# A margin for TensorE's order, small steps on two engines, 400 unread products and earlier squares in an attention and two-MoE kernel

## The chip, the cores and the metric

The kernel runs on one core of one Trainium2 chip. The metric is the device time of one execution in microseconds; the median of three runs is given. Engines are called TensorE (PE, its weight loads PEld), VectorE (DVE), ScalarE (ACT) and GpSimd (POOL). SyncE (SP) issues the DMAs.

## The reference, cut to what matters

```python
# q, k, v: (4, 8, 576, 64); M_prev: (4, 8, 64, 64); tokens: 4 * 576 = 2304, model width 8 * 64 = 512
scores = where(causal, -1e9, scale * q @ k^T)
local = softmax(scores) @ v
q_p = where(q > 0, q, exp(q) - 1) + 1
mem_out = (q_p @ M_prev) / (q_p . z_prev + 1e-6)
x = g * mem_out + (1 - g) * local            # g = sigmoid(beta); x: (2304, 512)

h = x @ w_in                                 # MoE1, 512 -> 2048
x = softplus(h) @ w_out                      # 2048 -> 512

h = x @ w_in2                                # MoE2
P = a0 + a1*h + a2*h^2 + a3*h^3
Q = 1 + |b0|*|h| + |b1|*h^2
out = (P / (Q + 1e-6)) @ w_out2
```

## The kernel before, in words

**Stages.** Attention is cut into seven passes, each a batch with a range of its query tiles (`PASSES`). A pass is cut into units of two or four heads: u0 to u5 in passes 0 to 2, which are computed in f32, and 16 later units in fp16 (a high and a low half for each value). Per unit there are scores, the mask with the row maximum, the exponential, a transpose of the probabilities and the product with v ("av" below), and beside it the memory part. The tokens that a pass finishes make a block for MoE1. Block 0's products are in f32 (128x256, 128 of them for each of the two matrices), those of the others in fp16 with three products for one. MoE2 follows over all 2304 tokens in 96 groups: 12 products of 384 columns for h (h1), then 9 of 512 columns for the output (h2).

**Weights.** The inputs are 64-bit values that the kernel takes apart on the chip: a piece of 128x512 comes as two words for each value, and VectorE makes f32 of it with one tensor_scalar and two scalar_tensor_tensor on integers (`bits`). There are 16 pieces of w_in and 16 of w_out for MoE1 (`w1_bits`, with `w1_load` for the DMA). Then `w1_stage2` squares every piece on ScalarE, with the sum of squares of each partition into a column of wacc1, takes the maximum of these with `w_scale` (which ends in `pmax`: a reduction over lanes on GpSimd and a product on TensorE) and splits each piece into two fp16 halves. The squares' unread full output goes to a_t[1]. In the trace these tiles are named w (pieces that belong to w_14 and others by number in the order), arena (one large buffer of which most tiles are cut), a (a_t), tiny (columns of scalars), gg and iog (the gate), bank (PSUM) and mask.

**What sets the order.** Every operation is first recorded in a program with a list of engines that can do it (`flex` records several) and a rank (`key`, for TensorE `pkey`; low goes first). `Program.order` then runs a list scheduler over a table of costs (`cost`, `LATENCY`, `BIAS`): each engine has a heap `wait` of operations whose inputs come at a known modelled time, and a heap `ready` ordered by rank. An operation that several engines may do goes to the one whose modelled end, weighted with the bias, is earliest. `emit` issues all instructions in the order that comes out, which is fixed then; so nearly all of them bear the line of `emit`: L426 before, L437 after (L439 and L441 before are L450 and L452 after). Each engine takes its own in that order and waits where an input isn't there. The ranks for TensorE: attention first by unit, then MoE1 by block, then MoE2 by group. `pmax` has the first rank of all; 120 unread products on a zero mask (`WARM`, rank 1e6) have the last.

VectorE and GpSimd share a port in the planner's costs: an operation of one gets longer while the other is working (`port`, `PORT`).

Of the kernel before, what the change touches and what calls it, by code (L numbers as in the profile page):

```python
# [24 lines left out]
LAG = 3  # L25
NLOW = 4

# [19 lines left out]
WARM = 120  # L47
FA32 = 3
# [81 lines left out]
def cost(eng, name, kw):  # L130
# [15 lines left out]
    if eng == "DVE":  # L146
        if name == "reciprocal":
            return 67 + 6.2 * n
        one = name in ("tensor_scalar", "tensor_copy", "memset") and not psum
        aps = sum(is_ap(kw.get(k)) for k in ("scalar", "scalar1", "scalar2", "scale"))  # L150
        return (77 if name == "tensor_tensor_reduce" else 67) + (0.52 if one else 1.042) * n + 62 * aps
# [19 lines left out]
class Program:  # L171
# [151 lines left out]
    def order(self):  # L323
# [13 lines left out]

        def release(o):
            o.cand = {"BULK"} if o.bulk and "SP" in o.alts else set(o.alts)
            for e in o.cand:  # L340
                heapq.heappush(wait[e], (o.ready, o.pkey if e == "PE" else o.key, o.idx))
# [8 lines left out]
        while len(done) < len(self.ops):  # L350
            best = None
            for e in engines:
                trim(ready[e])
                trim(wait[e])
                if ready[e]:
                    s = max(free[e], now[e])
                elif wait[e]:
                    s = max(free[e], wait[e][0][0])
                else:
                    continue  # L360
# [5 lines left out]
            now[e] = s  # L366
            while wait[e] and wait[e][0][0] <= s:
                _, k, i = heapq.heappop(wait[e])
                heapq.heappush(ready[e], (k, i))
# [6 lines left out]
            if t > s:  # L376
                heapq.heappush(wait[e], (t, k, i))
# [20 lines left out]
            if e in port and e in o.port:  # L398
# [57 lines left out]
def attn_moe_moe2(ctx, tc, q, k, v, m_prev, z_prev, beta, w1i, w1o, w2i, w2o, ca, cb, out):  # L456
# [123 lines left out]
    def tt(out, in0, in1, op, eng="VG"):  # L580
        kw = dict(out=out, in0=in0, in1=in1, op=op)
        P.flex(*[(e, "tensor_tensor", kw) for e, c in ((V, "V"), (G, "G")) if c in eng])

    def stt(out, in0, scalar, in1, op0, op1):
        V.scalar_tensor_tensor(out=out, in0=in0, scalar=scalar, in1=in1, op0=op0, op1=op1)
# [11 lines left out]
    def ts(out, in0, s1, s2, op0, op1=None):  # L597
# [3 lines left out]
        V.tensor_scalar(**kw)  # L601
# [765 lines left out]
    def w1_bits(which, pc):  # L1367
        r = w1_raw(which, pc)
        dst = w1_place(which, pc + 2, True)
        bits(r, dst.bitcast(U32))  # L1370

    def w1_stage2(which):
        for pc in range(16):
            A.activation(out=a_t[1][:, 768:1280], in_=w1_place(which, pc + 2, True), func=AF.Square, accum_out=wacc1[which][:, pc:pc + 1])
# [49 lines left out]
    for _ in range(WARM):  # L1424
        PE.matmul(out=bank[0][:, 0:256], lhsT=mask[:, 0:128], rhs=mask[:, 0:256], start=True, stop=True)
    early = EARLY(load, units, consts, lambda: batch_load(passes[0]))
# [273 lines left out]
```

## Time and profile before

| what | value |
|---|---|
| median of 3 runs | 1016.39 us (1015.85 to 1101.25) |
| profiled execution | 1013.9 us |
| its span, first to last instruction | 1011.8 us |
| mean granted clock of TensorE, as a share of full speed | 0.976 |
| busy: TensorE / VectorE / ScalarE / GpSimd | 94% / 86% / 71% / 47% |
| instructions on VectorE / ScalarE / GpSimd | 2182 / 1636 / 579 |

The times of stages and instructions below come from the profiled execution alone, whose own time is 2.1 us more than its span. A share of busy time is a mean over stages with different limits; the views by stage, the timelines of an engine and the lists of what it waited for are what tells them apart. An f32 product shows as two records in the trace.

### The profile page before, as it was taken

How to read it: one execution, taken by the hardware profiler on the slowest of the kernel's cores; microseconds unless marked ns; L12 is line 12 of the kernel's file. 1: busy time of each engine (PE TensorE's matmuls, PEld its weight loads, DVE VectorE, ACT ScalarE, POOL GpSimd, SP SyncE). 2: the span in 40 equal slices, each digit the busy share in tenths (PEclk: the TensorE clock that was granted, in tenths of full speed). 3: DMA queues.
4: the chain of work that ended last, by engine and by line, in shares of the span. 5: the costliest groups of instructions: out<-in, count | busy, mean ns of one | idle time of the engine just before them, and what ended most of it. 6: DMA issues, size and time to landing. Idle time of an engine off the chain costs nothing.

```text
span 1011.8 us, 22830 instructions
## 1 busy us (share of the span) xinstructions
PE 950.3 (94%) x8386; PEld 689.3 (68%) x8386; DVE 872.1 (86%) x2182; ACT 722.2 (71%) x1636; POOL 474.7 (47%) x579
## 2 busy tenths in 40 slices
PE   7776899999899999999799999999999999999998
PEld 6454587788788888888689899555555555555553
DVE  4989899899798888889769997988979889898886
ACT  4765896768676768777554444888788787887875
POOL 2434397933253343244225342564555455555443
PEclk9777899999999999999999999999999999999999
DMA  9997247688699888989997542000101000000000
GB/s 233 302 239 203 53 88 140 134 147 167 128 177 187 142 156 160 174 170 198 216 289 248 197 150 60 10 1 32 32 1 64 1 32 32 1 33 1 32 1 31
DMA packets 247584, 117.89 MB, mean 117 GB/s; under 512 B 218928, under 2 KB 225072, under 8 KB 247472
## 3 DMA queue, kind: packets, MB, share of 16 engines
q1 hardware_dynamic: 247472, 116.44, 50.6%
q8 instruction: 65, 1.06, 0.5%
q14 instruction: 47, 0.39, 0.1%
HBM read 63.45 MB, written 13.63 MB: 76 GB/s over the span
## 4 chain that ended last, share of the span: by engine, by line
PE 37%; DVE 9%; DMA 7%; issue 2%; POOL 2%; ACT 1%; SPq 0%; POOLq 0%; DVEq 0%; ACTq 0%
PE bank L426 37%; DVE arena L426 5%; DMA arena<-arena 2%; DVE bank L426 1%; DMA arena<-in_moe_w_out_dram 1%; DMA arena<-in_moe_w_in_dram 1%; POOL arena L426 1%; DMA arena<-a 1%; DVE gr L426 1%; ACT arena L426 1%; DMA w2d<-a 1%; DVE a L426 1%; DVE tiny L426 0%; DMA arena<-in_q_dram 0%; SPq L426 0%
## 5 line engine op out<-in xcount | busy, mean ns | idle before, releaser
L426 PE MATMUL bank<-arena,w 128*128 128x160 f16 (+3 forms) x4448 | 406.2, 252 | 0.7 <-ACT arena L426 0.7
L426 PE MATMUL bank<-arena 128*128 128x384 f16 (+10 forms) x2820 | 351.6, 300 | 35.5 <-DVE tiny L426 9.4
L426 PEld LDWEIGHTS <-w 128*128 128x128 f16 x4224 | 328.9, 98 | 21.9 <-issue 6.5
L426 ACT ACTIVATE arena<-bank,tiny 128x384 f32<-128x384 f32 (+9 forms) x518 | 276.7, 583 | 62.5 <-PE bank L426 38.7
L426 PEld LDWEIGHTS <-arena 128*128 128x128 f16 (+1 forms) x2464 | 164.6, 104 | 120.3 <-issue 26.8
L426 POOL TENSOR_TENSOR arena<-arena 128x384 f32<-128x384 f32 (+6 forms) x171 | 174.3, 1022 | 152.5 <-ACT arena L426 104.2
L426 PE MATMUL bank<-arena,gr 128*128 128x512 f16 x864 | 201.5, 379 | 0.6 <-POOL gr L426 0.4
L426 ACT ACTIVATE bank<-bank,tiny 128x512 f32<-128x512 f32 (+5 forms) x200 | 106.8, 539 | 61.4 <-PE bank L426 32.1
L426 PEld LDWEIGHTS <-gr 128*128 128x128 f16 x864 | 84.3, 98 | 93.5 <-POOL gr L426 1.3
L426 POOL TENSOR_TENSOR gr<-arena,gr 128x384 f16<-128x384 f32 x96 | 90.6, 944 | 102.1 <-issue 81.9
L426 DVE SCALAR_TENSOR_TENSOR arena<-bank,tiny,arena 128x384 f16<-128x384 f32 (+4 forms) x200 | 113.7, 594 | 18.7 <-ACT arena L426 17.8
L426 POOL TENSOR_SCALAR arena<-arena,tiny 128x512 f16<-128x512 f32 (+9 forms) x100 | 77.1, 777 | 63.5 <-DVE tiny L426 22.9
L426 DVE SCALAR_TENSOR_TENSOR arena<-arena,tiny 128x512 f16<-128x512 f32 (+5 forms) x102 | 87.0, 869 | 7.1 <-POOL arena L426 6.0
L426 DVE SCALAR_TENSOR_TENSOR bank<-bank,tiny,lt 128x384 f32<-128x384 f32 x96 | 59.7, 621 | 35.0 <-ACT lt L426 33.1
L426 DVE TENSOR_SCALAR tiny<-tiny 128x1 f32<-128x1 f32 (+10 forms) x404 | 73.7, 207 | 11.4 <-ACT bank L426 8.7
L426 ACT ACTIVATE lt<-arena,qe 128x384 f32<-128x384 f32 x96 | 58.9, 614 | 30.5 <-POOL arena L426 28.8
L426 DVE CUSTOM_DVE_ANT_0 bank<-bank,mask,tiny 128x384 f32<-128x384 f32 (+3 forms) x112 | 66.8, 606 | 7.3 <-PE bank L426 6.2
L426 PEld LDWEIGHTS bank<-arena 128*128 128x128 f32 (+3 forms) x380 | 40.5, 181 | 40.6 <-ACT arena L426 12.4
L426 DVE SCALAR_TENSOR_TENSOR arena<-arena,qe,lt 128x384 f32<-128x384 f32 x96 | 67.5, 703 | 0.0
L426 POOL TENSOR_SCALAR tiny<-tiny 128x1 f32<-128x1 f32 (+2 forms) x71 | 19.8, 279 | 96.2 <-DVE tiny L426 89.1
L426 DVE SCALAR_TENSOR_TENSOR bank<-arena,tiny,bank 128x384 f32<-128x384 f32 x96 | 59.2, 617 | 2.2 <-ACT arena L426 0.8
L426 ACT ACTIVATE arena<-arena 128x512 f32<-128x512 f32 (+4 forms) x67 | 42.4, 634 | 26.2 <-DVE arena L426 18.8
(118 smaller groups left out, 1010.6 us busy)
## 6 DMA issues: line engine op xcount, KB each, us to landing
arena<-in_moe_w_out_dram SPq DMA_DIRECT2D x32, 512.0 KB, 4.6
arena<-in_moe_w_in_dram SPq DMA_DIRECT2D x24, 512.0 KB, 5.6
arena<-in_k_dram SPq DMA_DIRECT2D x44, 128.0 KB, 3.6
arena<-in_v_dram SPq DMA_DIRECT2D x44, 128.0 KB, 3.2
arena<-arena SPq DMA_DIRECT2D x32, 160.0 KB, 3.1
arena<-x2d SPq DMA_DIRECT2D x6, 768.0 KB, 4.4
out_dram<-arena SPq DMA_DIRECT2D x18, 256.0 KB, 2.1
w<-in_moe_w_in_dram SPq DMA_DIRECT2D x8, 512.0 KB, 9.7
```

Source lines behind the costliest of these rows:

```text
L426: fn(**{k: (v.fn() if isinstance(v, Lazy) else v) for k, v in kw.items()})
```

## The change

It has four parts.

1. `SLACK`, 300 ns, for TensorE alone: in the planner an operation enters the heap by rank only once its inputs have been there for 300 ns in the model. If none has, the one whose inputs came first is taken, without a margin.
2. `ts`, `tt` and `stt` let GpSimd do steps of at most 16 elements a partition, when all operands lie outside PSUM and the operation is an add, subtract, mult, max or min; a scalar_tensor_tensor becomes two instructions there. The modelled cost of such a step on VectorE changes, and the port is charged for operations over 400 ns alone.
3. `FILL`: 400 products of 64 columns on the zero mask into a part of bank[7] that nothing reads, at the last rank.
4. The squares of the first weights are recorded in `w1_bits`, behind each piece's conversion (with `KEY_SQ` = 0 added to its rank), instead of in `w1_stage2`.

```diff
+SLACK = 300.0
+POOL_OPS = (ALU.add, ALU.subtract, ALU.mult, ALU.max, ALU.min)
+KEY_SQ = 0.0
+FILL = 400
...
+        if n <= 16:
+            return 95 + 85 * aps
...
+        slack = {e: SLACK if e == "PE" else 0.0 for e in engines}
...
-                heapq.heappush(wait[e], (o.ready, o.pkey if e == "PE" else o.key, o.idx))
+                heapq.heappush(wait[e], (o.ready + slack[e], o.pkey if e == "PE" else o.key, o.idx))
...
-                    s = max(free[e], wait[e][0][0])
+                    s = max(free[e], now[e], wait[e][0][0] - slack[e])
...
+            if not ready[e] and slack[e]:
+                _, k, i = heapq.heappop(wait[e])
+                heapq.heappush(ready[e], (k, i))
...
-                heapq.heappush(wait[e], (t, k, i))
+                heapq.heappush(wait[e], (t + slack[e] + 0.01, k, i))
...
-            if e in port and e in o.port:
+            if e in port and e in o.port and dur > 400:
...
     def tt(out, in0, in1, op, eng="VG"):
         kw = dict(out=out, in0=in0, in1=in1, op=op)
+        if width(out) <= 16 and op in POOL_OPS and not any(is_psum(v) for v in (out, in0, in1)):
+            eng = "VG"
...
     def stt(out, in0, scalar, in1, op0, op1):
+        if width(out) <= 16 and not any(is_psum(v) for v in (out, in0, in1, scalar)) and span(out) != span(in1):
+            P.flex(
+                (V, "scalar_tensor_tensor", dict(out=out, in0=in0, scalar=scalar, in1=in1, op0=op0, op1=op1)),
+                [
+                    (G, "tensor_scalar", dict(out=out, in0=in0, scalar1=scalar, scalar2=None, op0=op0)),
+                    (G, "tensor_tensor", dict(out=out, in0=out, in1=in1, op=op1)),
+                ],
+            )
+            return
...
-        V.tensor_scalar(**kw)
+        if width(out) > 16 or op0 not in POOL_OPS or op1 not in (None,) + POOL_OPS or any(is_psum(v) for v in (in0, s1, s2)):
+            V.tensor_scalar(**kw)
+        else:
+            P.flex((V, "tensor_scalar", kw), (G, "tensor_scalar", kw))
...
         dst = w1_place(which, pc + 2, True)
         bits(r, dst.bitcast(U32))
+        P.key += KEY_SQ
+        A.activation(out=a_t[1][:, 768:1280], in_=dst, func=AF.Square, accum_out=wacc1[which][:, pc:pc + 1])
 
     def w1_stage2(which):
-        for pc in range(16):
-            A.activation(out=a_t[1][:, 768:1280], in_=w1_place(which, pc + 2, True), func=AF.Square, accum_out=wacc1[which][:, pc:pc + 1])
...
+    for _ in range(FILL):
+        PE.matmul(out=bank[7][:, 256:320], lhsT=mask[:, 0:128], rhs=mask[:, 0:64], start=True, stop=True)
```

What the planner makes of it can be seen in the engines' queues. On VectorE, 264 instructions fewer stand in the queue of the changed kernel (1918 instead of 2182), on GpSimd 288 more (867 instead of 579).

VectorE, the conversion of weights w_14 (pieces 12 and 13 of w_in) in the start, before: it ends behind the maxima (ISA, from bank with mask) of a later set of scores. The places are 246 to 256 of the queue.

```order
L426 ISA arena,tiny<-bank_74,mask 128x128
L426 ISA tiny 128x1
L426 ISA arena,tiny<-bank_73,mask 128x128
L426 ISA tiny 128x1
L426 ISA arena,tiny<-bank_74,mask 128x128
L426 ISA tiny 128x1
L426 TENSOR_SCALAR tiny<-bank_75 128x1
L426 SCALAR_TENSOR_TENSOR w_14_92<-w_15_93,w_14_92 128x512
L426 TENSOR_SCALAR arena<-arena 128x512
L426 TENSOR_SCALAR w_15_93<-arena 128x512 x2
L426 SCALAR_TENSOR_TENSOR w_15_93<-arena,w_15_93 128x512 x4
```

And now (places 159 to 168), with the maxima of an earlier set ahead of it:

```order
L437 ISA tiny 128x1
L437 TENSOR_SCALAR w_9_87<-arena 128x512 x2
L437 SCALAR_TENSOR_TENSOR w_9_87<-arena,w_9_87 128x512 x4
L437 SCALAR_TENSOR_TENSOR tiny<-tiny,iog 128x4
L437 TENSOR_SCALAR w_11_89<-arena 128x512
L437 SCALAR_TENSOR_TENSOR w_14_92<-w_15_93,w_14_92 128x512
L437 SCALAR_TENSOR_TENSOR w_11_89<-arena,w_11_89 128x512
L437 SCALAR_TENSOR_TENSOR w_14_92<-w_15_93,w_14_92 128x512
L437 SCALAR_TENSOR_TENSOR tiny<-tiny,iog 128x4
L437 SCALAR_TENSOR_TENSOR w_11_89<-arena,w_11_89 128x512
```

The steps on w_14 have moved forward, past the attention's steps that stood ahead of them: the first of the three from place 227 to 138, the last from 253 to 166. Up to u5's last reciprocal the queue has 284 instructions instead of 287.

TensorE, the end of u5's attention (bank_75<-arena 64x256 and 64x128 are its av products, bank_72 to 74 its transposes) and block 0's f32 products (bank_70 and bank_71, with weights w_6 and w_8), before:

```order
L426 MATMUL bank_74<-arena 128x128 x3
L426 MATMUL bank_72<-arena 128x128 x3
L426 MATMUL bank_75<-arena 64x256 x4
L426 MATMUL bank_75<-arena 64x128 x2
L426 MATMUL bank_75<-arena 64x256 x4
L426 MATMUL bank_75<-arena 64x128 x2
L426 MATMUL bank_70<-arena,w_6_84 128x256 x8
L426 MATMUL bank_75<-tiny,one 128x5
L426 MATMUL bank_71<-arena,w_8_86 128x256 x4
```

And now:

```order
L437 MATMUL bank_75<-arena 64x128 x2
L437 MATMUL bank_72<-arena 128x128 x3
L437 MATMUL bank_73<-arena 128x128 x3
L437 MATMUL bank_74<-arena 128x128 x3
L437 MATMUL bank_70<-arena,w_6_84 128x256 x4
L437 MATMUL bank_72<-arena 128x128 x3
L437 MATMUL bank_75<-arena 64x256 x4
L437 MATMUL bank_75<-arena 64x128 x2
L437 MATMUL bank_71<-arena,w_8_86 128x256 x4
L437 MATMUL bank_75<-tiny,one 128x1
L437 MATMUL bank_75<-arena 64x256 x4
L437 MATMUL bank_75<-arena 64x128 x2
```

Three groups of four f32 products have moved ahead of u5's last two av groups, and the rest follows behind the last. In the new queue all of the 400 added products stand ahead of the first f32 product of block 0: 123 of them between the 120 warm ones, and then runs of 30, 14, 13, 156, 39 and 25. The run of 156 stands behind u0's av.

GpSimd, its first work on loaded data (gg and iog are the gate, arena,gg a product of it with memory), before:

```order
L439 MEMSET arena 128x2x64
L426 TENSOR_TENSOR arena<-arena,gg 128x512
L426 TENSOR_TENSOR arena<-arena 128x512 x2
L426 TENSOR_SCALAR tiny<-tiny 128x4
L426 TENSOR_TENSOR arena<-arena,tiny 128x512
L426 TENSOR_TENSOR arena<-arena,gg 128x512
L426 TENSOR_TENSOR arena<-arena 128x512
```

And now:

```order
L450 MEMSET arena 128x2x64
L437 TENSOR_SCALAR gg<-gg 128x8
L437 TENSOR_SCALAR fb<-bb 128x2
L437 TENSOR_SCALAR fr<-bb 128x2
L437 TENSOR_SCALAR iog<-gg 128x8
L437 TENSOR_TENSOR arena<-arena,gg 128x512
L437 TENSOR_SCALAR iog_104<-iog 128x8
L437 TENSOR_TENSOR arena<-arena 128x512
L437 TENSOR_SCALAR tiny<-tiny 128x8 x2
L437 TENSOR_TENSOR arena<-arena,tiny 128x512
L437 TENSOR_SCALAR tiny<-tiny 128x4 x2
L437 TENSOR_TENSOR tiny<-tiny,iog 128x4
```

Small steps on the gate, and then on tiny, have come between the products of 128x512.

At the passage from MoE1 to MoE2, the queue of TensorE had all of MoE1's products and then four h1 groups in a row; now h1 groups stand between the last six groups of MoE1's second matrix, and the first h2 group comes behind them.

## Rows read from the trace of the kernel before

**Rows 1.** TensorE's line of the page's first part: busy, share, instructions (load, then product)

```profile
PE 950.3 (94%) x8386; PEld 689.3 (68%) x8386; DVE 872.1 (86%) x2182; ACT 722.2 (71%) x1636; POOL 474.7 (47%) x579
```

**Rows 2.** Busy time by stage; columns: stage, its length, engines, TensorE's granted clock, DMA

```profile
16.00:118.80 102.80, 77.95 (x471) 52.17 (x468) 92.27 (x276) 69.96 (x213) 38.63 (x35) 0.78 0.76 216
118.80:200.00 81.20, 77.84 (x514) 64.52 (x511) 74.60 (x185) 65.92 (x155) 68.71 (x72) 1.00 0.57 116
200.00:460.00 260.00, 251.25 (x3016) 215.99 (x3017) 222.68 (x717) 192.59 (x481) 99.11 (x171) 0.99 0.88 160
460.00:540.00 80.00, 69.63 (x1063) 64.48 (x1058) 64.70 (x166) 45.95 (x110) 27.94 (x38) 1.00 1.04 246
540.00:640.00 100.00, 95.72 (x1294) 91.43 (x1292) 89.29 (x191) 50.41 (x112) 37.49 (x43) 1.00 0.44 141
640.00:1000.00 360.00, 360.00 (x1942) 189.87 (x1941) 317.38 (x616) 287.11 (x552) 194.82 (x202) 1.00 0.05 18
```

**Rows 3.** TensorE's timeline of the start: start, us, instruction, idle time before it

```profile
27.65 2.08 PE L426 MATMUL bank<-arena 64*128 64x256 f32 x8 [2.64 <-ACT arena L426]
...
53.24 1.99 PE L426 MATMUL bank<-arena,w 128*128 128x256 f32 x8
...
57.95 3.38 PE L426 MATMUL bank<-arena,w 128*128 128x256 f32 x8
...
117.47 1.45 PE L426 MATMUL bank<-arena 64*64 64x256 f32 x12 [0.54 <-ACT arena L426]
118.85 3.72 PE L426 MATMUL bank<-arena,w 128*128 128x256 f32 x16
...
125.27 14.08 PE L426 MATMUL bank<-arena,w 128*128 128x256 f32 x64
```

**Rows 4.** TensorE's waits from 118.8 to 640 us: sum, times, longest

```profile
PE bank L426 <- DVE arena L426: 8.2, 10, 1.6
PE bank L426 <- POOL tiny L426: 7.7, 8, 2.0
PE bank L426 <- DMA arena<-arena: 7.1, 8, 2.2
```

**Rows 5.** TensorE's timeline at the passage from MoE1 to MoE2

```profile
630.17 7.96 PE L426 MATMUL bank<-arena 128*128 128x384 f16 x48
639.49 2.11 PE L426 MATMUL bank<-arena 128*128 128x384 f16 x12 [1.36 <-DVE arena L426]
```

**Rows 6.** Small steps by shape (busy, mean ns), and two neighbours in VectorE's timeline

```profile
L426 DVE TENSOR_SCALAR tiny<-tiny 128x1 f32<-128x1 f32 x136 | 23.4, 182 | 2.2 <-ACT bank L426 1.8
...
L426 POOL TENSOR_SCALAR tiny<-tiny 128x1 f32<-128x1 f32 x59 | 15.4, 261 | 78.4 <-DVE tiny L426 72.0 <-DVE tiny L441 5.2
...
69.89 0.16 DVE L426 TENSOR_SCALAR tiny<-tiny 128x8 f32<-128x8 f32 x1
69.97 0.41 DVE L426 TENSOR_SCALAR w<-arena 128x512 uint32<-128x512 uint32 x1
```

**Rows 7.** GpSimd's timeline of the start

```profile
18.42 1.04 POOL L426 TENSOR_TENSOR arena<-arena,gg 128x512 f32<-128x512 f32 x1 [12.52 <-DVE gg L441]
...
36.56 0.25 POOL L426 TENSOR_SCALAR tiny<-tiny 128x4 f32<-128x4 f32 x1 [5.38 <-DVE tiny L426]
...
42.82 11.47 POOL L426 TENSOR_TENSOR arena<-arena,gg 128x512 f32<-128x512 f32 x1 [3.10 <-DMA arena<-in_M_prev_dram]
...
57.70 0.68 POOL L426 TENSOR_SCALAR tiny<-tiny 128x4 f32<-128x4 f32 x1 [2.19 <-DVE tiny L426]
```

**Rows 8.** ScalarE's squares from 16 to 200 us

```profile
L426 ACT ACTIVATE a<-w 128x512 f32<-128x512 f32 x26 | 16.2, 624 | 0.7 <-DVE w L426 0.4
```

**Rows 9.** Runs of fp16 products in TensorE's timeline

```profile
599.79 15.80 PE L426 MATMUL bank<-arena,w 128*128 128x160 f16 x226
...
180.62 2.08 PE L426 MATMUL bank<-arena 128*64 128x320 f16 x58
```

**Rows 10.** Busy time in a stretch of the start, columns as in Rows 2

```profile
89.00:106.00 17.00, 10.41 (x43) 7.39 (x43) 17.00 (x57) 11.63 (x36) 7.69 (x12) 0.50 0.57 154
```

## The prediction

> **What bounds the kernel now.** I read the page first, then the busy time by stage, then TensorE's timeline of the start and its waits in the rest. On the page TensorE is busy for 94% of the span, so most of any gain has to come out of its idle time: 1011.8 - 950.3 = 61.5 us [rows 1]. The table by stage says where that lies [rows 2]. From 640 to 1000 us, in MoE2, TensorE is busy for 360.00 of 360.00 us; nothing there can become shorter unless its own products do, and the change does not touch them. From 16 to 118.8 us it is idle for 102.80 - 77.95 = 24.9 us. Here VectorE is the full engine, 92.27 of 102.80 us, and ScalarE is not (69.96). From 118.8 to 640 us TensorE's idle time is 3.4 + 8.8 + 10.4 + 4.3 = 26.8 us over four rows, most dense from 460 to 540 us. The remaining 10 us lie before the first data and in the last 12 us.
>
> So the kernel has three regimes: a start of 119 us paced by the f32 attention with VectorE full, a middle in which MoE1's products fill TensorE but for short waits, and a tail that is TensorE alone.
>
> **The change part by part.**
>
> *Block 0's f32 products among the attention.* In the timeline of the start, the last f32 product of u5's attention begins at 117.47 us, and only then, from 118.85 us, do the rest of block 0's f32 products run [rows 3]. In the new order three groups of four of these, 12 products, stand between the av and transpose products of u5, ahead of its last av. Their weights (w_14) get their last conversion step on VectorE at places 138 to 166 of its queue instead of 227 to 253, so they should be there. A product shows as two records: 64 records took 14.08 us, so one product takes 0.44 us, and 12 take 5.3 us. If they run in what is now idle time, the whole 5.3 us leaves the stretch behind 118.85. The floor is 0: then the attention gets longer by as much. The ceiling is VectorE's idle time in the stretch, 102.80 - 92.27 = 10.5 us, since its work there hardly changes: 287 instructions up to u5's reciprocal before, 284 now, of which 13 fewer are small and 1 more piece of weights is converted. I take -5.3, from 0 to -10.5.
>
> *The margin of 300 ns.* Up to now TensorE's static order took the product of highest rank as soon as the planner believed its operands ready; where the planner was early, the whole queue stood still. With the margin, ready MoE1 products stand ahead of it. From 118.8 to 640 us the waits that this can cover are 10 on VectorE's arena, 8 on GpSimd's tiny and 8 on the DMA inside arena, 26 in all and 23.0 us [rows 4]. A wait of 2 us is not cured by moving one product back by 300 ns, and the attention's chain gets later by the same margin. The ceiling is 26 x 0.3 = 7.8 us, the floor 0. I take -3.0, nearer the floor, because the mean wait is 23.0/26 = 0.88 us, three times the margin.
>
> *The passage from MoE1 to MoE2.* Before, four h1 groups (48 products) run by themselves from 630.17 us behind the last MoE1 product, and then there is a gap of 1.36 us until VectorE has delivered for the next [rows 5]. In the new order the first h1 groups stand between the last six MoE1 groups, so their activation starts earlier and the gap should be covered: -1.4, from 0 to -1.4.
>
> *Small steps on GpSimd.* VectorE loses 264 instructions, GpSimd gains 288. On VectorE a small step lasts 182 ns, but the next one starts 80 ns behind it (69.89 and 69.97 us) [rows 6]: 264 x 0.08 = 21 us less on VectorE, of 872.1. On GpSimd one takes 261 ns [rows 6], and 288 of them are 75 us on top of 474.7, some 54% of the span. VectorE isn't the bound from 118.8 us on, so its 21 us buy nothing there directly; TensorE's queue of MoE1 products hides them. What could cost is the length of a chain of small steps. Duration alone is 261 - 182 = 79 ns for a step. Then comes contention: the same GpSimd product took 1.04 us at 18.42 and 11.47 us at 42.82, while VectorE was converting weights, and a small step took 0.25 us at 36.56 and 0.68 at 57.70 [rows 7]. From 118.8 to 200 us GpSimd is already busy for 68.71 of 81.20 us [rows 2], so a small step there also queues behind products of most of a microsecond. The cover is the reserve of MoE1 products. Exposed steps I take at four a unit, over the two units nearest the start: 8 x 0.3 = +2. The floor is -2: VectorE's shorter queue in the start, 13 steps at 0.08, and one wait of 1 us less behind it. The ceiling is +12: four steps in each of the 6 first units at 0.43 + 0.08 us. I take +2, because VectorE keeps most small steps in the start (13 move there).
>
> *Squares piece by piece.* The 32 squares move forward in ScalarE's queue. Each takes 624 ns [rows 8], 20 us in all without their accumulator reads. Half now fall into the start, where ScalarE is busy for 69.96 of 102.80 us; the cover is its 32.8 us of idle time. The scale of the first weights can come earlier, but the fp16 block that needs it is only reached after 164 us, so 0. Without the cover each square in front of an exponential would cost its 0.6 us.
>
> *The 400 fills.* They are 128x64 products that nobody reads. No row shows one; the nearest rows are 128x160 products with a weight load each, 226 in 15.80 us, 70 ns, and 58 of attention's fp16 products (64 columns among others), 2.08 us, 36 ns [rows 9]. So 400 take 14 to 28 us. All stand before block 0's first product: 123 among the 120 warm products, the rest in runs of 30, 14, 13, 156, 39 and 25. TensorE is idle for 24.9 us in the start and 5.7 us before it, so they fit, but the queue is in order: whatever is ready behind a run waits for its end. The run of 156 takes 5.6 to 10.9 us. They can also gain: from 89 to 106 us the granted clock was 0.50, that is the lower of the two levels, and eight f32 records took 3.38 us at 57.95 against 1.99 us at 53.24 [rows 3, 10]. A kernel whose TensorE is less idle before such stretches may keep the upper level there. But in that same stretch VectorE is busy for 17.00 of 17.00 us, so shorter products would wait for VectorE all the same. I take 0, from -5 (half of the 10.41 us of products at the lower clock) to +9 (the run of 156 at 70 ns, less 2 us of idle time that it would fill).
>
> [...]
>
> **Sum.** -5.3 - 3.0 - 1.4 + 2 + 0 + 0 = -7.7 us. The profiled execution took 1013.9 us (span 1011.8 and 2.1 around it), so a profiled run of the new kernel should take about 1006. The median of the three runs was 1016.39, 2.5 us above the profiled one; the change gives 1016.4 - 7.7 = 1008.7 us. That is 0.8%, and about 2% is what a measurement of this kernel can tell from no change.
>
> **The rivals.**
>
> *Nothing comes of it (1013 to 1018).* The 12 products move, but the attention that feeds passes 1 to 6 is the true pace: what MoE1 finishes early is idle again in the 460 to 540 us stretch, where waits for a DMA inside arena already stand, 8 of them [rows 4]. For it: VectorE is 90% full in the start and its work stays. Against it: from 200 to 460 us TensorE is busy for 251.25 of 260, so MoE1 has its own queue of ready work. The sum is then 0 to -2 for the passage: about 1015.
>
> *The start and most waits go (some 993).* The fills keep the clock up and the earlier weights let VectorE close its gaps: -10.5 in the start, -7.8 from the margin, -5 by the clock, -1.4 at the passage, together -24.7, and 992. For it: each term is within its bounds. Against it: all must come at once, and two share the same idle time.
>
> *Slower: GpSimd's small steps stretch every unit's chain (1037 or more).* 16 units follow u5. If on each of them four small steps that TensorE's next product waits for go to GpSimd, and each costs the 0.08 us of duration and the 0.43 us of starvation seen at 57.70 us [rows 7], the chains grow by 16 x 4 x 0.51 = 33 us. It decides only where the reserve of MoE1 products is used up. It becomes slower by over 2% when 20.3 + 7.7 = 28 us of the 33 come through. For it: 8 waits on GpSimd's tiny, up to 2 us, stand in the trace already. Against it: these are 7.7 us in 521, and the units' chains run beside products with 94% of TensorE's time used.
>
> *Fills in the way (about 1020).* If the runs of 156 and 39 are still going when u1's and u2's products are ready, they push those chains back: 195 x 0.070 = 13.7 us, less the 2.6 us that TensorE waited there anyhow (the gap at 27.65 us) [rows 3], is +11.1, and 1008.7 + 11.1 = 1019.8. For it: the runs stand in front of those products. Against it: the products that a run delays are ready later than the planner believed just as often as earlier. [...]
>
> **How the numbers follow.** The forecast, a gain of 1 to 16 us (1000 to 1015), has a chance of 0.50; nothing comes of it 0.20; the big gain 0.18; slower by GpSimd 0.08; fills in the way 0.04. Of the big gain 0.02 stays within 2% and of the forecast 0.02 goes beyond, so faster by over 2% is 0.18, slower by over 2% 0.08, within 2% 0.74. The terms' bounds reach from 1016.4 - 10.5 - 7.8 - 1.4 - 2 - 5 = 990 to 1016.4 + 12 + 9 = 1037; both ends want every term at its end, so the upper one is cut to where fills and small steps cost half, 1016.4 + 10.5 = 1027. Range 990 to 1027.
>
> **What would show it.** In the new profile: f32 128x256 products between u5's 64x256 products, and the stretch behind u5 shorter by 5 us; waits from 118.8 to 640 us of about 20 us instead of 26.8; VectorE near 850 us and GpSimd near 550; h1 products from before MoE1's end, no gap of 1.4 us behind. Runs of 128x64 products followed by a product that had long been ready would show the fills in the way. The prediction is wrong if u5's last av comes later than 119 us with VectorE no longer full (then the start is paced by small steps or fills), or if it comes more than 8 us earlier.

## The result: slower by one per cent, and the profile after

The changed kernel takes 1027.26 us (median of 5 runs, 1025.4 to 1028.55), the kernel before 1016.39. The ratio is 1.0099, with a 95% interval from 1.0075 to 1.0123: slower, just above the upper end of the range, where 1008.7 had been forecast. One execution of the kernel before, of 1101.25 us, was in a second, slower state and is left out of the ratio. The profiled execution took 1027.75 us with a span of 1025.0, 13.2 us more than before.

TensorE's line of the page's first part comes first; it answers to [rows 1].

```profile
PE 959.1 (94%) x8786; PEld 700.5 (68%) x8786; DVE 852.2 (83%) x1918; ACT 712.8 (70%) x1618; POOL 574.7 (56%) x867
```

TensorE's idle time is 1025.0 - 959.1 = 65.9 us, 4.4 more than before, and its busy time has grown by 8.8 us, in which the fills stand. VectorE has lost 19.9 us of work, and GpSimd, with 288 instructions more, has gained 100.0 us: 347 ns for each by the difference of the totals, where the prediction had 261. The busy time by stage, in the columns and stages of [rows 2]:

```profile
16.00:118.80 102.80, 80.28 (x794) 60.36 (x793) 93.26 (x258) 64.13 (x199) 40.04 (x53) 0.82 0.74 212
118.80:200.00 81.20, 76.91 (x492) 60.91 (x491) 66.49 (x166) 63.17 (x149) 68.69 (x85) 0.98 0.48 95
200.00:460.00 260.00, 245.64 (x2925) 210.88 (x2924) 201.17 (x559) 187.56 (x474) 142.30 (x293) 0.99 0.87 159
460.00:540.00 80.00, 72.88 (x1058) 65.94 (x1057) 66.36 (x160) 51.97 (x126) 39.29 (x67) 1.00 1.05 231
540.00:640.00 100.00, 95.78 (x1338) 92.47 (x1338) 85.75 (x162) 47.61 (x107) 53.05 (x74) 1.00 0.49 173
640.00:1000.00 360.00, 356.48 (x1977) 190.94 (x1976) 315.81 (x560) 278.91 (x532) 216.93 (x274) 1.00 0.06 19
```

In the start TensorE's idle time is 22.5 us, 2.3 less than before, since fills stand in it. From 118.8 to 640 us it is 4.3 + 14.4 + 7.1 + 4.2 = 30.0 us, against 26.8; and MoE1 isn't over at 640 us, so 3.5 us of idle time follow behind. From the first h2 product to the end it takes 1025.0 - 658.49 = 366.5 us, against 1011.8 - 641.43 = 370.4 before. That is no gain: seven h1 groups now stand ahead of that product instead of five, and two groups of 1.95 us each are the difference. MoE2 itself has lost and gained nothing.

TensorE's timeline of the start, as in [rows 3]:

```profile
39.30 4.72 PE L437 MATMUL bank<-mask 128*128 128x64 bf16 x156
...
99.88 2.35 PE L437 MATMUL bank<-arena 128*128 128x128 f32 x8 [7.63 <-DVE tiny L437]
...
116.70 1.99 PE L437 MATMUL bank<-arena,w 128*128 128x256 f32 x8
...
121.05 1.89 PE L437 MATMUL bank<-arena,w 128*128 128x256 f32 x8
...
124.58 1.99 PE L437 MATMUL bank<-arena,w 128*128 128x256 f32 x8
...
126.81 1.45 PE L437 MATMUL bank<-arena 64*64 64x256 f32 x12
...
130.42 1.99 PE L437 MATMUL bank<-arena,w 128*128 128x256 f32 x8
```

The run of 156 fills took 4.72 us, 30 ns each, under the 36 ns that was the lower bound. At 99.88 us TensorE had waited 7.63 us for VectorE, and the last av products of u5 begin at 126.81 us instead of 117.47. The 12 products of block 0 that were to move stand ahead of them, in three rows of 5.87 us together; so 9.34 - 5.87 = 3.5 us were lost in the start, and the rest of the 13.2 us behind it, ahead of MoE2. The wait comes with the order of VectorE's queue, whose timeline shows the maxima of u4's scores (CUSTOM_DVE_ANT_0) apart from each other:

```profile
92.62 0.41 DVE L437 CUSTOM_DVE_ANT_0 a<-bank,mask 128x256 f32<-128x256 f32 x1
...
94.70 0.41 DVE L437 CUSTOM_DVE_ANT_0 a<-bank,mask 128x256 f32<-128x256 f32 x1
...
95.98 0.88 DVE L437 SCALAR_TENSOR_TENSOR w<-arena,w 128x512 uint32<-128x512 uint32 x1
96.79 1.15 DVE L437 SCALAR_TENSOR_TENSOR arena<-arena 128x512 uint32<-128x512 uint32 x1
...
99.40 0.41 DVE L437 CUSTOM_DVE_ANT_0 a<-bank,mask 128x256 f32<-128x256 f32 x1
```

The third and the fourth have 4.35 us of weight pieces between them. ScalarE's exponentials for these scores then wait 11.78 us, the last of it for a small step on GpSimd (ScalarE's timeline):

```profile
100.55 0.51 ACT L437 ACTIVATE a<-a,tiny 128x256 f32<-128x256 f32 x1 [11.78 <-POOL tiny L437]
```

That looked like the whole cause at first; experiment e3 speaks against it. TensorE's waits from 126 to 660 us, as in [rows 4], and the passage to MoE2, as in [rows 5]:

```profile
PE bank L437 <- DVE arena L437: 13.4, 13, 2.6
PE bank L437 <- POOL tiny L437: 9.6, 10, 2.0
PE bank L437 <- DMA arena<-arena: 4.0, 4, 1.7
```

```profile
649.04 2.11 PE L437 MATMUL bank<-arena 128*128 128x384 f16 x12 [2.57 <-DVE arena L437]
...
656.54 2.11 PE L437 MATMUL bank<-arena 128*128 128x384 f16 x12 [0.95 <-DVE arena L437]
658.49 3.83 PE L437 MATMUL bank<-arena,gr 128*128 128x512 f16 x17
```

The waits on the DMA are fewer (8 to 4), but those on VectorE's arena have become 13.4 us instead of 8.2, and those on GpSimd's tiny 9.6 instead of 7.7. The gaps at the passage stand in the sums on VectorE's arena; without them these are 9.9 and 6.8 us. At the passage the h1 groups do stand between MoE1's last products, and still there are two gaps, 2.57 and 0.95 us, for one of 1.36.

Small steps on GpSimd by shape, as in [rows 6]:

```profile
L437 POOL TENSOR_SCALAR tiny<-tiny 128x1 f32<-128x1 f32 x157 | 51.0, 326 | 88.8 <-DVE tiny L437 65.8 <-ACT bank L437 14.7 <-DVE tiny L452 3.5
L437 POOL TENSOR_SCALAR tiny<-tiny 128x2 f32<-128x2 f32 x64 | 29.4, 460 | 16.5 <-ACT bank L437 9.9 <-DVE tiny L437 4.8
```

The planner counts 240 ns and 0.83 ns for each element of such a step. They took 326 and 460. One chain with such steps can be followed through three engines. GpSimd's, VectorE's and TensorE's timelines, and the busy time of TensorE ahead of the wait and behind it:

```profile
380.79 1.14 POOL L437 TENSOR_TENSOR arena<-arena 128x192 f32<-128x192 f32 x2 [1.59 <-DVE arena L437]
382.61 0.20 POOL L437 TENSOR_SCALAR tiny<-tiny 128x6 f32<-128x6 f32 x1 [0.68 <-DVE tiny L437]
383.31 0.55 POOL L437 CROSS_LANE_REDUCE tiny<-tiny 128x5 f32<-128x5 f32 x1 [0.50 <-DVE tiny L437]
```

```profile
381.96 0.56 DVE L437 TENSOR_REDUCE tiny<-arena 128x6 f32<-128x384 f32 x1 [0.85 <-POOL arena L437]
382.85 0.19 DVE L452 RECIPROCAL tiny<-tiny 128x6 f32<-128x6 f32 x1 [0.33 <-POOL tiny L437]
383.08 0.16 DVE L437 TENSOR_REDUCE tiny<-tiny 128x2 f32<-128x6 f32 x1
```

```profile
376.75 5.12 PE L437 MATMUL bank<-arena,w 128*128 128x192 f16 x60
383.92 0.38 PE L437 MATMUL bank<-tiny,one 1*128 1x5 f32 x2 [2.04 <-POOL tiny L437]
384.23 1.86 PE L437 MATMUL bank<-arena,w 128*128 128x192 f16 x12
```

```profile
376.75:381.87 5.12, 5.12 (x65) 4.89 (x60) 1.57 (x3) 3.76 (x8) 3.29 (x7) 1.00 1.06 170
384.50:388.00 3.50, 3.50 (x17) 2.01 (x15) 1.53 (x7) 0.00 (x0) 2.77 (x5) 0.51 0.44 98
```

VectorE's row maximum at 381.96 us came 0.85 us late, as GpSimd's arena products ended late; then the chain goes to GpSimd for a small step (382.61), back to VectorE for two (382.85, 383.08) and to GpSimd again for the reduction over lanes (383.31). TensorE's product for it has the first rank of all, so the MoE1 products behind it in the queue stood still for 2.04 us. Then the granted clock fell to 0.51, near the lower of its two levels: 12 products took 1.86 us, 155 ns each, against 60 in 5.12 us, 85 ns, ahead of the wait. So this wait cost TensorE its 2.04 us and, by an estimate from the 3.5 us at half the clock, 1.7 us more. In this chain the small step (0.20 us) and the reduction (0.55 us) themselves were no longer than planned; what was late came in with the arena products, which had waited 1.59 us for VectorE, and each change of engine passed it on. Small steps that are longer than planned show in e5 below.

### The profile page after: what moved, and what is told of

It is laid out like the page before. It is cut to its first block, busy times and chain, and to the rows that moved or that the text cites. A ratio compares the mean times of both kernels' runs of the same rounds, so it can differ in the third digit from the quotient of the medians.

```text
span 1025.0 us, 23668 instructions
## 1 busy us (share of the span) xinstructions
PE 959.1 (94%) x8786; PEld 700.5 (68%) x8786; DVE 852.2 (83%) x1918; ACT 712.8 (70%) x1618; POOL 574.7 (56%) x867
## 3 DMA queue, kind: packets, MB, share of 16 engines
q8 instruction: 68, 1.11, 0.5%
## 4 chain that ended last, share of the span: by engine, by line
PE 32%; DVE 9%; DMA 3%; POOL 3%; issue 2%; ACT 1%; POOLq 0%; SPq 0%; DVEq 0%; ACTq 0%
PE bank L437 32%; DVE arena L437 5%; POOL arena L437 2%; DMA arena<-in_moe_w_in_dram 2%; DVE bank L437 1%; POOL tiny L437 1%; ACT arena L437 1%; DMA arena<-in_moe_w_out_dram 1%; DVE gr L437 1%; DVE a L437 1%; DVE tiny L437 1%; DMA arena<-x2d 1%; DMA x2d<-arena 0%; ACT bank L437 0%; ACT lt L437 0%
## 5 line engine op out<-in xcount | busy, mean ns | idle before, releaser
L437 PE MATMUL bank<-arena 128*128 128x384 f16 (+9 forms) x2820 | 349.5, 299 | 35.0 <-DVE tiny L437 14.2
L437 ACT ACTIVATE arena<-bank,tiny 128x384 f32<-128x384 f32 (+6 forms) x520 | 274.7, 583 | 64.3 <-PE bank L437 41.5
L437 POOL TENSOR_TENSOR arena<-arena 128x384 f32<-128x384 f32 (+6 forms) x163 | 166.4, 1023 | 136.1 <-ACT arena L437 105.4
L437 POOL TENSOR_SCALAR tiny<-tiny 128x1 f32<-128x1 f32 (+6 forms) x280 | 101.2, 362 | 141.8 <-DVE tiny L437 100.7
L437 ACT ACTIVATE bank<-bank,tiny 128x384 f32<-128x384 f32 (+5 forms) x200 | 107.4, 541 | 69.1 <-POOL tiny L437 30.9
L437 DVE SCALAR_TENSOR_TENSOR arena<-bank,tiny,arena 128x512 f16<-128x512 f32 (+4 forms) x200 | 113.9, 594 | 22.4 <-ACT arena L437 20.3
L437 POOL TENSOR_SCALAR arena<-arena,tiny 128x512 f16<-128x512 f32 (+10 forms) x104 | 81.6, 790 | 41.5 <-DVE arena L437 23.8
L437 DVE CUSTOM_DVE_ANT_0 bank<-bank,mask,tiny 128x384 f32<-128x384 f32 (+4 forms) x112 | 66.5, 607 | 6.4 <-PE bank L437 5.1
L437 ACT ACTIVATE arena<-arena 128x512 f32<-128x512 f32 (+3 forms) x65 | 41.0, 633 | 24.5 <-DVE arena L437 15.6
L437 DVE SCALAR_TENSOR_TENSOR arena<-arena,bank 128x384 f32<-128x384 f32 x96 | 52.8, 550 | 2.1
```

Source lines behind the costliest of these rows:

```text
L437: fn(**{k: (v.fn() if isinstance(v, Lazy) else v) for k, v in kw.items()})
```

## The experiments

Ratios are against the kernel before, on the same chip, with their 95% intervals. Each kernel of the first four undoes one of the four parts.

```diff
-FILL = 400                      # e1
+FILL = 0
-SLACK = 300.0                   # e2
+SLACK = 0.0
-        if n <= 16: return 95 + 85 * aps          # e3: cost, port rule and the three flex branches out
-            if e in port and e in o.port and dur > 400:
+            if e in port and e in o.port:
-        A.activation(..., func=AF.Square, ...)    # e4: out of w1_bits, back into w1_stage2
```

**e1**, no fills.

> The changed kernel without the 400 fills (FILL = 0), all else as changed. Theory A (the fills cost, by their place in TensorE's queue and by what the planner makes of VectorE's queue behind them: the maxima of u4's scores stand with 10 weight pieces' steps between them, 1 without the fills): u5's last av product comes before 120 us again instead of 126.8, and the time is 1014 to 1019. Theory B (GpSimd's small steps lengthen the chains): 1023 to 1028, as the changed kernel. Theory C (any new order costs or gains some us without a pattern): somewhere from 1010 to 1030.

**e2**, no margin.

> The changed kernel with a margin of 0 in the planner, fills, small steps and squares as changed. Theory A: u4's maxima still have 13 weight steps between them, so the start stays slow (last av of u5 after 124 us) and the time is 1022 to 1030. Theory D (the margin is what costs, since it puts MoE1 products ahead of a product of the attention that is ready): 1014 to 1019.

**e3**, small steps as before.

> The changed kernel with small steps, their cost and the port's rule as in the kernel before; fills, margin and squares as changed. Theory A: 7 weight steps still stand between u4's maxima; 1019 to 1026, a little better than the changed kernel. Theory B: the loss is gone, 1012 to 1018, and TensorE's waits on GpSimd's tiny fall from 12 (11.3 us) back to 8.

**e4**, squares as before.

> The changed kernel with the squares of the first weights back in one piece ahead of their scale; all else as changed. Theories A, B and D: the squares are hidden on ScalarE, 1024 to 1030, within 0.3% of the changed kernel. Theory C: some us off to either side.

| run | median us | ratio | interval |
|---|---|---|---|
| e1 | 1031.01 | 1.0157 | 1.0122 to 1.0193 |
| e2 | 1028.26 | 1.0142 | 1.0106 to 1.0178 |
| e3 | 1010.21 | 0.9968 | 0.9942 to 0.9993 |
| e4 | 1027.57 | 1.0136 | 1.0098 to 1.0174 |

Theory A falls: without fills the kernel is no better, and u5's last av, for which it had less than 120 us, begins at 137.09. Theory D falls by e2. The loss goes with the small steps, and with them alone. Theory B has the direction right, but its figures were too narrow: e1 lies above its 1023 to 1028, e3 below its 1012 to 1018, and e3's waits on GpSimd's tiny fell to 4 (3.5 us), not to 8. What speaks against the start as the main cause is e3's own timeline of TensorE:

```profile
95.04 1.12 PE L435 MATMUL bank<-arena 128*128 128x128 f32 x4 [6.63 <-DVE tiny L435]
...
104.66 1.22 PE L435 MATMUL bank<-arena 64*128 64x128 f32 x6 [5.16 <-DVE tiny L435]
...
130.84 1.45 PE L435 MATMUL bank<-arena 64*64 64x256 f32 x12
```

It has two such waits, 6.63 and 5.16 us, and its last av products come at 130.84 us, later than in the changed kernel. Yet it is faster than the kernel before: 28 of the f32 products moved ahead in it, not 12, and used 13.0 us of the 13.4. In the changed kernel 3.5 us of the start weren't made up.

The next four ask whether the part is enough by itself, and which half of it, the work on GpSimd or the planner's new cost and port rule. Each is the changed kernel with other edits undone: e5 has the second part alone, e6 its rules without the offer to GpSimd, e7 the offer without the rules, e8 only margin and squares.

```diff
-        if width(out) <= 16 and op in POOL_OPS and ...:          # e6: in tt and stt; the test in ts is made always true
+        if False:
-        if n <= 16: return 95 + 85 * aps                         # e7
-            if e in port and e in o.port and dur > 400:
+            if e in port and e in o.port:
```

**e5**, the second part alone.

> The kernel before with the second part alone: small steps on VectorE or GpSimd with their cost and the port's rule. No fills, no margin, squares as before. Theory B (this part makes the loss, as the runs without one part suggest: the three that keep it gave 1.014 to 1.016, the one without it 0.997): 1.010 to 1.020 of the kernel before, TensorE's waits on GpSimd's tiny above 11 us, MoE1's last product after 645 us. Theory E (the loss needs the margin or the squares beside it): 0.995 to 1.004.

**e6**, its rules without the steps.

> The changed kernel, with the planner's new cost of a small step and the port charged over 400 ns alone, but no small step offered to GpSimd. Theory B1 (it is the work on GpSimd that costs): 0.994 to 1.002 of the kernel before. Theory B2 (it is the planner's view of port and cost that misplaces steps): 1.010 to 1.018.

**e7**, the steps without its rules.

> The changed kernel, with small steps offered to GpSimd, but planned with the old cost and the old port rule. Theory B1: 1.008 to 1.020 of the kernel before, by how many steps the planner still gives to GpSimd. Theory B2: 0.995 to 1.003.

**e8**, margin and squares.

> The changed kernel without fills and without small steps: margin and squares alone, the planner's old rules. If the gain of the run without small steps (0.997) is the margin's: 0.993 to 0.999. If it is the fills': 1.000 to 1.005. Theory C (orders scatter without a pattern): outside both.

| run | median us | ratio | interval |
|---|---|---|---|
| e5 | 1027.81 | 1.0127 | 1.0082 to 1.0171 |
| e6 | 1017.09 | 1.0016 | 0.9995 to 1.0037 |
| e7 | 1017.52 | 1.0022 | 1.0003 to 1.0042 |
| e8 | 1011.48 | 0.9953 | 0.9934 to 0.9972 |

The second part alone makes the loss (theory B). Neither of its halves does: each by itself is worse than e3 by about 0.5%, and both together by 1.3%. e6 came out as B1 had it and e7 as B2 had it, so neither half is the cause by itself; most of the loss needs steps on GpSimd and a planner that thinks them short. The margin (with the squares, e8) gains 0.5% where the small steps stay as before; beside them it shows no gain (e1 1.0157, e5 1.0127). In e5 the longest such wait can be read off GpSimd's timeline, and behind it VectorE's and TensorE's:

```profile
575.22 2.15 POOL L437 TENSOR_SCALAR tiny<-tiny 128x1 f32<-128x1 f32 x3 [0.28 <-DVE tiny L437]
577.47 1.11 POOL L437 TENSOR_SCALAR tiny<-tiny,fb 128x1 f32<-128x1 f32 x2
...
579.33 0.94 POOL L437 TENSOR_SCALAR tiny<-tiny 128x1 f32<-128x1 f32 x2
...
582.34 0.76 POOL L437 CROSS_LANE_REDUCE tiny<-tiny 128x1 f32<-128x1 f32 x1 [1.02 <-DVE tiny L437]
```

```profile
579.39 0.75 DVE L437 SCALAR_TENSOR_TENSOR arena<-arena,tiny 128x512 f16<-128x512 f32 x1 [1.45 <-POOL arena L437]
```

```profile
583.15 0.58 PE L437 MATMUL bank<-tiny,one 1*128 1x1 f32 x2 [3.81 <-POOL tiny L437]
```

Seven small steps took 2.15 + 1.11 + 0.94 us, 0.60 each with the gaps between them, where 0.24 was planned. With the larger ones between them they keep VectorE waiting for 1.45 us; what VectorE has to give to the reduction at 582.34 comes late, and TensorE stands still for 3.81 us.

The next four test this reading (theory F) against the rival that long chains cost however they are planned (theory G).

```diff
             dur = o.alts[e][0]
+            if e == "POOL" and dur < 300:       # e9: after the engine is chosen
+                dur += 200
-                heapq.heappush(wait[e], (o.ready + slack[e], ...                             # e10, and e11 on e8
+                heapq.heappush(wait[e], (o.ready + slack[e] + (1500 if e == "PE" and o.pkey == -1e6 else 0), ...
-            if e in port and e in o.port and dur > 400:                                      # e12
+            if e in port and e in o.port:
```

**e9**, 200 ns more for GpSimd's short steps.

> The changed kernel, where the planner, once it has chosen the engine, counts 200 ns more for every GpSimd step that it takes to be under 300 ns. 329 of the changed kernel's 368 small steps stay on GpSimd. Theory F (the planner believes that small steps there end earlier than they do, 0.24 us against 0.35 measured on average, so TensorE's queue stands still at products that wait for GpSimd, the maxima's products above all): 1.000 to 1.005 of the kernel before, waits on GpSimd's tiny under 8 us. Theory G (the longer chains over GpSimd cost, however they are planned): 1.008 to 1.016.

**e10**, 1500 ns more of margin for the maxima's products.

> The changed kernel with another 1500 ns of margin for the products of pmax alone (those that spread a maximum over the lanes, which have the first rank of all). Theory F: most of the loss hangs on these waits and on the lower clock behind them, so 0.999 to 1.005 of the kernel before, waits on GpSimd's tiny under 4 us. Theory G: the waits move from these products to those that need their result, 1.008 to 1.016.

**e11**, the same on e8.

> Margin and squares alone (the run that gave 0.995) with another 1500 ns of margin for the products of pmax. Theory F: a little more of the same, since 4.1 us of waits on GpSimd's tiny are left: 0.990 to 0.995. Theory G or no effect: 0.994 to 0.999.

**e12**, the old port rule.

> The changed kernel with the old rule for the port (every step is charged for the other engine's work), and the new cost of small steps. If it is the port rule that makes the planner too early for GpSimd: 1.000 to 1.005. If it is the number of steps on GpSimd (377 small ones here, 368 in the changed kernel, 322 where cost and rule were old and the ratio 1.002): 1.009 to 1.016.

| run | median us | ratio | interval |
|---|---|---|---|
| e9 | 1008.24 | 0.9918 | 0.9888 to 0.9948 |
| e10 | 1026.51 | 1.0121 | 1.0088 to 1.0155 |
| e11 | 1020.38 | 1.0059 | 1.0036 to 1.0082 |
| e12 | 1017.11 | 1.0027 | 0.9996 to 1.0059 |

e9 is better than I expected, and faster than both kernels, though its GpSimd does nearly the work of the changed kernel (808 instructions against 867, 553.0 us against 574.7). That speaks against G. The number of small steps on GpSimd doesn't decide it either: 329 here, 322 in e7 and 377 in e12, which are both slower. The added time also falls to the 19 reductions over lanes of 128x1, which are planned at 285 ns. Its waits of TensorE behind the start, and its busy time by stage, in a profiled execution of 1002.86 us, the fastest of its seven:

```profile
PE bank L439 <- DVE arena L439: 9.5, 10, 2.4
PE bank L439 <- POOL tiny L439: 2.9, 2, 1.8
PE bank L439 <- DMA arena<-arena: 2.6, 4, 1.0
```

```profile
118.80:200.00 81.20, 77.20 (x509) 63.04 (x508) 70.15 (x181) 65.53 (x153) 70.31 (x76) 1.00 0.56 104
200.00:460.00 260.00, 250.87 (x3057) 218.16 (x3056) 205.10 (x587) 193.03 (x488) 138.25 (x281) 1.00 0.86 165
460.00:540.00 80.00, 74.87 (x1125) 68.53 (x1123) 66.59 (x163) 51.42 (x119) 39.44 (x54) 1.00 1.07 265
540.00:640.00 100.00, 100.00 (x1260) 90.95 (x1258) 91.47 (x173) 59.72 (x130) 56.20 (x81) 1.00 0.36 122
```

From 460 to 640 us the idle time has gone from 11.3 us (changed kernel) to 5.1, and the granted clock is 1.00 in every stage behind the start. e10 shows where my reading was too narrow. The waits on GpSimd's tiny do shrink, but the time doesn't:

```profile
PE bank L438 <- DVE arena L438: 17.9, 23, 2.5
PE bank L438 <- DMA arena<-arena: 7.2, 11, 1.4
...
PE bank L438 <- POOL tiny L438: 2.3, 4, 0.9
```

The lateness turns up at VectorE's arena, 23 waits of 17.9 us. F's forecast for e10 failed, and G's (1.008 to 1.016, the waits move) came true, though not by the length of the chains, as e9 shows. I take it that the chain is late and not the product that shows it first. And e11 says that holding these products back costs 1.1% in a kernel that was well planned: both expectations for it failed. e12 says that the port rule is the larger half of the rules: with it, the planner charges a GpSimd step for VectorE's work beside it again, and 1.0099 has become 1.0027 with as many steps on GpSimd. e7, with the old cost as well, is no different (1.0022).

e9's gain could still have been a lucky order. The last six runs ask that: a control that shifts ties in the kernel before by 0.01 ns (e13), 100 and 400 ns in place of 200 (e14, e15), 200 ns in the kernel before (e16), and 200 ns in two other slow versions, e1 (e17) and e4 (e18).

```diff
-                heapq.heappush(wait[e], (t, k, i))          # e13, on the kernel before
+                heapq.heappush(wait[e], (t + 0.01, k, i))
-                dur += 200                                  # e14 (e15: 400)
+                dur += 100
             dur = o.alts[e][0]                              # e16 before, e17 on e1, e18 on e4
+            if e == "POOL" and dur < 300:
+                dur += 200
```

**e13**, ties shifted in the kernel before.

> The kernel before, with 0.01 ns added in the planner to the time at which an operation that found its PSUM bank held is looked at again. It asks for nothing else, but many rows of the queues change places. Theory C (any new order scatters): 1.005 or more, or 0.995 or less. Theory F: 0.996 to 1.004.

**e14**, 100 ns.

> The changed kernel, the planner counting 100 ns more for GpSimd's short steps (200 ns gave 0.992, none 1.010 to 1.013). Theory F (an honest duration cures it, and 241 + 100 is the measured mean): 0.992 to 1.002. Theory C: no order by the added time, so 1.008 to 1.016 is as likely.

**e15**, 400 ns.

> The same with 400 ns more. Theory F: the waits on GpSimd stay away, 0.990 to 1.000. Theory C: anywhere from 0.990 to 1.016.

**e16**, 200 ns in the kernel before.

> The kernel before, none of the change in it, the planner counting 200 ns more for GpSimd's short steps. Theory F (only 75 small steps are there to be late): 0.992 to 1.001, mostly by the 8 waits on GpSimd's tiny (7.7 us). Theory C: anywhere from 0.990 to 1.010.

**e17**, 200 ns on e1.

> The changed kernel without fills (1.016 without the added time), the planner counting 200 ns more for GpSimd's short steps. Theory F: at least 0.8% less than without, 0.990 to 1.008. Theory C: by chance up or down, 1.005 to 1.020 as likely as below.

**e18**, 200 ns on e4.

> The changed kernel with the squares in one piece (1.014 without the added time), the planner counting 200 ns more for GpSimd's short steps. Theory F: at least 0.8% less than without, 0.990 to 1.006. Theory C: by chance up or down, 1.005 to 1.020 as likely as below.

| run | median us | ratio | interval |
|---|---|---|---|
| e13 | 1015.33 | 0.9998 | 0.9981 to 1.0015 |
| e14 | 1019.91 | 1.0027 | 1.0005 to 1.0050 |
| e15 | 1011.92 | 0.9952 | 0.9922 to 0.9982 |
| e16 | 1023.14 | 1.0067 | 1.0044 to 1.0090 |
| e17 | 1012.53 | 0.9963 | 0.9937 to 0.9990 |
| e18 | 1009.09 | 0.9929 | 0.9900 to 0.9958 |

With 0, 100 and 200 ns the changed kernel goes 1.0099, 1.0027, 0.9918, and 400 ns is a little worse than 200. From none to 200 ns, three versions fell by 1.8% (the changed kernel), 1.9% (e1 to e17) and 2.1% (e4 to e18). Three falls of one size are hardly chance in the order, and the tie control, a single one, moved nothing. TensorE's idle time from u5's last av to the first h2 product, in the profiled executions, goes the same way:

| run | idle us | with 200 ns | idle us |
|---|---|---|---|
| changed | 33.5 | e9 | 18.3 |
| e1 | 35.8 | e17 | 18.6 |
| e4 | 35.6 | e18 | 18.0 |

In the kernel before it is 26.8. In e17 u5's last av begins at 133.64 us, still later than in e3, and the kernel is faster than the one before all the same.

Two expectations failed. In the kernel before, the same 200 ns cost 0.7% (e16). So there is a scatter of that size between orders, or an overcharge where few steps are on GpSimd; which of the two isn't settled. And F, which wants an honest duration, had e14 at 1.002 at most. The tensor_scalar steps from tiny to tiny took 362 ns on average in the changed kernel, so 100 ns more than the planned 241 comes nearest to the mean, and 200 ns lies above it; yet 200 ns is better by 1.1%. So the cure is more than the mean. Whether it works as a reserve against the longer ones among the steps, or by the fewer steps that go to GpSimd, no run here separates.

## Why the prediction was wrong

**The step that failed** is the term for the small steps, +2 us with a ceiling of +12. Alone they cost 1.27% of 1015.5 us (the kernel before, beside e5), 12.9 us (8.3 to 17.4); beside margin and squares 1.0157 - 0.9953 = 2.0%, 21 us. Three things in it were wrong. It took 261 ns for a step, the mean of the 59 that GpSimd had then, and used the 0.68 us of 57.70 [rows 7] for the ceiling and the rival alone; by the totals an added instruction took 347 ns, a third more. It took the reserve of MoE1 products as cover. In a queue of fixed order the reserve covers only what the planner expects: where it thinks a step done, the product that needs it stands ahead of the reserve, and the reserve waits too. And it doesn't speak of the new rules (the cost of a small step, the port over 400 ns): it put an error of the planned time at nothing, without a reason. e9, e12, e14, e17 and e18 show that most of the loss hangs on it; how much of it is the step's duration and how much the reserve isn't separated.

The rival "slower by GpSimd's steps" named the engine and the starvation, at 0.08, but had the mechanism as chains that grow by their own length. With nearly as many steps in the chains and longer planned times, e9 gains 0.8%.

One reading that it leaned on for contention doesn't hold. The product of 11.47 us at 42.82 [rows 7] took 1.04 to 1.28 us at this place in 17 of the 20 traces, among them e8's, where VectorE converts weights beside it as before (GpSimd's timeline):

```profile
42.36 1.06 POOL L435 TENSOR_TENSOR arena<-arena,gg 128x512 f32<-128x512 f32 x1 [2.88 <-DMA arena<-in_M_prev_dram]
```

In e2 and e16 it took 8.60 and 10.82 us. What held it there is open. No term of the sum used it.

**Block 0's f32 products, -5.3.** The order was as read, and the products ran there. But u5's last av came 9.34 us later for 5.87 us of products, so the term came out at an estimated +3.5, beyond its floor of 0. In e3 the two nearly cancel (13.4 for 13.0 us). The sign named for it, the last av later than 119 us, came, but with VectorE as full as before (93.26 of 102.80 us): its queue's order paced the start.

**The margin, -3.0 (0 to -7.8).** Right by itself: e8 gives 0.47% of 1015.5 us, 4.8 us (2.8 to 6.7), and its squares are worth nothing by e4. The three waits named shrink in e8 from 23.0 to 18.0 us (10.8, 4.1 and 3.1), as forecast. Beside the small steps no such gain shows.

**The passage, -1.4.** Wrong in the changed kernel: two gaps, 3.5 us, for one of 1.36.

**Squares, 0.** Right: e4 and the changed kernel have intervals that overlap.

**Fills, 0 (-5 to +9).** Right: e3 with fills 0.9968, e8 without 0.9953, e9 with 0.9918, e17 without 0.9963. The rival that has them in the way fell with e1. In the run of 156 one took 30 ns. The Trainium skill ("TensorE: Matmul & The Clock Gate", section "Back-to-back issue gap") gives about 25 ns as the issue floor for a product of up to 64 columns by itself, which that run comes near. They do fill the start's idle time, and the granted clock of 16 to 118.8 us rose from 0.78 to 0.82; VectorE, at 93.26 of 102.80 us, was the pace all the same.

The busy time of VectorE, 852.2 us, and that of GpSimd, 574.7, came close to the forecast 850 and 550, though GpSimd's gain was 100 us and not 75. They decided nothing.

## What to carry to other kernels

In a kernel whose queues are fixed by a planner, a change of the planner's costs is a change of the kernel: price the error of each planned duration on the engine with the least certain times, at the engine that waits in order. Before a step is moved to a shared or starved engine, take its duration from the rows where the neighbour is busy, not from the mean; and when a whole family of waits appears, lengthen the planned time of the step that is late before moving the product that waits. Here 200 ns in one line turned 1.0099 into 0.9918; in the kernel before, with few such steps, the same line cost 0.7%, so it has to be measured.

## What the runs showed of the hardware

A small step on GpSimd has no fixed price. In the changed kernel one of 128x4 took 0.22 us, of 128x2 0.77 us at 375.69 us, and the two on fb in e5 0.50 us on average. Of the changed kernel's 340 small tensor_scalar steps there, the 240 beside which VectorE was busy for over 80% of their time took 417 ns on average, and the 68 with VectorE busy for under 20% took 257. The Trainium skill, "SBUF — State Buffer", section "SBUF: two separate sides", says that GpSimd and VectorE share a pair of ports by an exclusive lock: a GpSimd instruction and a VectorE instruction that reads two SBUF inputs, or runs in a two-port mode, block each other for a whole instruction. The two averages agree with it in kind, but no run here took VectorE's work away to show it.

A wait of TensorE can cost twice. Behind the wait of 2.04 us at 383.92 the clock stood at 0.51 for 3.5 us, in which its row counts 17 products. Most such waits aren't followed by it: in the changed kernel two of the twelve waits of over 1.2 us behind the start were, and e9 waited up to 2.4 us there and kept 1.00.
